# Longformer attention into a softplus layer: weights loaded in smaller pieces, the first batch's loads and the engines' sequence rearranged

## The chip, the core and the metric

The kernel runs on one core of one Trainium2 chip. The metric is the device time of the kernel in microseconds (us), median of three runs. Lower is better.

## What is computed

The reference is attention with a window and eight global positions, followed by two dense layers with a softplus between them. Cut to what matters:

```python
# q, k, v: [8 batches, 8 heads, 576 positions, 64], fp32
mask = np.abs(pos[:, None] - pos[None, :]) <= 32
mask = mask | is_global[:, None] | is_global[None, :]
scores = np.where(mask, q @ k.T / 8, -1e9)
attn = softmax(scores)
x = (attn @ v).transpose(0, 2, 1, 3).reshape(4608, 512)
g = softplus(x @ w_in)        # w_in  [512, 2048]
out = g @ w_out               # w_out [2048, 512], fp32 out
```

## The kernel before

**Tiles.** The 576 positions of a batch are 18 blocks of 32. Four blocks make a pair `n` (36 in all), four pairs make a tile `m` of 512 tokens (nine in all). For each pair TensorE computes the scores `s` (32 small matmuls on a divided array, L1085), the softmax runs on VectorE, ScalarE and GpSimd and ends in `pt`, the transposed probabilities (L1149). For each tile TensorE then computes `xo` (L1259: probabilities by values, and by `vg`, the global rows' part), which is copied to `xT` in bf16, and the dense layers `h` (L1294: 64 matmuls of 512 columns a tile) and `o` (L1305). The first tile is cut into three pieces of one, two and one pair, so that `h` starts on 128 tokens as soon as pair 0 is through. Work that is done once per batch: turning q and k (`tr`), choosing the global positions (`pick`), their scores `sg`, and `ov`, which gives `vg`.

**The start.** For the first batch, q and k come in parts (L522 full parts of 256 tokens, L526 the tail of 64 tokens in two transfers) on SyncE's queue. The values `vb` (L477, eight transfers) and the weights `w_in` (`weights_in`, L1356, eight transfers into four tiles `win0` to `win3`) and `w_out` (`weights_out`, L1360, four) go through GpSimd's queue, because they are cast to bf16 on the way. A transfer that is issued by an engine is an instruction in that engine's queue. Three gates order these transfers: `T["held"]` (L1373) is a one-element copy on GpSimd that waits for a part of q, so that `w_in` comes behind it; `follow` (L765) is a tiny transfer `trail` on SyncE that reads the last element of a weight tile and so waits for it, ahead of the second batch's parts (`win2`) and values (`wout0`); `T["landed"]` (L1437) is a copy that waits for a part of the second batch's k, ahead of `w_out`.

**The sequence.** A class `_Order` plans all work. The table `ORDER` fixes which job comes next and on which engine; the planner's constants (`SWITCH`, `SLOW`, `FETCH`, the `moves` of a transfer) give each job a planned time, by which the jobs of all engines are sorted when they are written out. Where TensorE has a planned gap in the first 34 us, `keep` fills it with matmuls on zeros (`warm`, L737). The planner also knows that TensorE's instructions are fetched in blocks:

```python
    BLOCK = 256
    ASK = 130
    NEED = 448
```

It takes it that a block of 256 instructions is asked for when instruction 130 (386, 642, ...) is reached and is needed at instruction 448 (704, 960, ...).

**The table of picks** (`make_pick`, L595 to L603) is used from the third batch on: VectorE clears it, makes three small tables and compares four times (L601).

## Time and profile before

| | |
|---|---|
| median of 3 runs | 331.63 us (331.45 to 332.01) |
| the profiled execution | 331.16 us, of which its span (first to last instruction) is 329.1 us |
| TensorE busy | 319.9 us (97%) |
| ScalarE, VectorE, GpSimd busy | 233.8, 219.9, 196.0 us |
| TensorE's granted clock, mean over the span | 0.995 |
| `warm` matmuls | 46 |

All times in the rows count from the first instruction of the span. PE is TensorE's matmuls, PEld its weight loads, DVE VectorE, ACT ScalarE, POOL GpSimd, SP SyncE; a small q behind a name is the engine's sequencer. In the chain of waits, "issue" is time in which the engine waited for nothing that the profile shows. Matmuls overlap, so a busy TensorE isn't one at its peak: start times show its pace.

### The profile page before, as it was taken

The numbers are of one execution on the slowest core, as the hardware profiler recorded it, in microseconds if no ns is written. First come the engines' busy times: TensorE is split into PE (matmuls) and PEld (weight loads), VectorE is DVE, ScalarE is ACT, GpSimd is POOL, SyncE is SP. The second block draws the span as 40 slices with busy tenths as digits, with TensorE's granted clock in tenths as the row PEclk, the third lists the DMA queues.
The fourth block names the chain that finished last, engine by engine and source line by source line (L and its number), as shares of the span: only waits on it lengthen the run. The fifth ranks groups of instructions, "written<-read, shape, count | busy, mean of one in ns | idle before, by whom it ended". The sixth has DMA issues, their size and how long they took to land.

```text
span 329.1 us, 12101 instructions
## 1 busy us (share of the span) xinstructions
PE 319.9 (97%) x5290; PEld 171.3 (52%) x5290; DVE 219.9 (67%) x386; ACT 233.8 (71%) x459; POOL 196.0 (60%) x175
## 2 busy tenths in 40 slices
PE   8878999999999999999999999999999999999996
PEld 3536876565555444544555445445544454454444
DVE  7796689847997799884995975378776970431000
ACT  5698879676798896488558857995749647914622
POOL 7827828996678567969587496738282927230000
PEclk9997999999999999999999999999999999999999
DMA  7998999999889899999999960370010012001002
GB/s 193 187 205 195 198 189 155 157 166 244 136 152 146 152 226 173 180 228 189 178 179 167 155 162 4 127 145 3 4 66 0 36 66 85 13 32 66 34 32 97
DMA packets 168796, 42.14 MB, mean 128 GB/s; under 512 B 153256, under 2 KB 165800, under 8 KB 168744
## 3 DMA queue, kind: packets, MB, share of 16 engines
q1 hardware_dynamic: 155928, 27.15, 46.8%
q0 software_dynamic: 10944, 11.08, 16.9%
q10 hardware_dynamic: 1872, 3.15, 2.5%
q8 instruction: 41, 0.67, 0.9%
q14 instruction: 11, 0.09, 0.1%
HBM read 36.71 MB, written 9.44 MB: 140 GB/s over the span
## 4 chain that ended last, share of the span: by engine, by line
PE 90%; DVE 2%; SPq 2%; DMA 2%; issue 1%; ACT 1%
PE o L1305 39%; PE h L1294 37%; PE xo L1259 4%; PE s L1085 4%; DMA stage<-in_q_dram 2%; PE ov L1005 2%; SPq L522 1%; PE pick L894 1%; SPq L526 1%; PE sg L976 1%; PE warm L737 1%; DVE qx L728 1%; PE tr L865 1%; DVE m L1100 1%; PE pick L907 1%
## 5 line engine op out<-in xcount | busy, mean ns | idle before, releaser
L1305 PE MATMUL o<-wout,g 128*128 128x512 bf16 (+1 forms) x592 | 138.3, 374 | 0.0
L1294 PE MATMUL h<-xT,win 128*128 128x512 bf16 (+3 forms) x768 | 137.8, 328 | 0.1
L1300 ACT ACTIVATE g<-h 128x512 bf16<-128x512 f32 (+3 forms) x192 | 84.5, 503 | 30.0 <-PE h L1294 27.0
L1140 POOL TENSOR_TENSOR pn<-st,rs 128x1024 bf16<-128x1024 f32 (+1 forms) x38 | 66.7, 1766 | 55.7 <-DVE rs L1134 49.9
L1294 PEld LDWEIGHTS <-win 128*128 128x128 bf16 x768 | 67.5, 99 | 59.6 <-issue 0.8
L1305 PEld LDWEIGHTS <-g 128*128 128x128 bf16 x592 | 55.9, 98 | 60.7 <-ACT g L1300 1.0
L1108 POOL TENSOR_TENSOR st<-st,m 128x1024 f32<-128x1024 f32 x32 | 60.2, 1894 | 27.1 <-DVE m L1102 27.0
L1089 DVE TENSOR_TENSOR st<-s,mask 128x512 f32<-128x512 f32 x64 | 41.1, 677 | 18.6 <-PE s L1085 18.4
L1132 DVE TENSOR_REDUCE sm<-st 128x8 f32<-128x1024 f32 x32 | 38.5, 1203 | 14.8 <-ACT st L1125 14.6
L1102 DVE TENSOR_REDUCE m<-st 128x8 f32<-128x1024 f32 x32 | 37.9, 1209 | 0.3
L728 ACT COPY osb<-o 128x512 f32<-128x512 f32 (+1 forms) x30 | 17.2, 577 | 22.6 <-PE o L1305 20.2
L1125 ACT ACTIVATE st<-st 128x1024 f32<-128x1024 f32 x32 | 32.7, 1052 | 0.3
L1149 DVE STREAM_TRANSPOSE pt<-pn 128x512 int32<-128x512 int32 x36 | 24.5, 690 | 5.2 <-POOL pn L1140 5.1
L728 ACT CAST xT<-xo 128x512 bf16<-128x512 f32 (+3 forms) x28 | 11.7, 467 | 18.8 <-PE xo L1259 18.8
L728 DVE CAST xT<-xo 128x512 bf16<-128x512 f32 (+3 forms) x20 | 11.3, 601 | 17.5 <-PE xo L1259 17.4
L1300 ACT ACT_TABLE_LOAD x15 | 19.2, 1283 | 1.7 <-PE h L1294 1.5
L1125 ACT ACT_TABLE_LOAD x14 | 18.0, 1283 | 0.7 <-ACT osb L728 0.4
L725 POOL TENSOR_SCALAR qb<-stage 128x1152 bf16<-128x1152 f32 (+2 forms) x15 | 16.8, 1126 | 2.2 <-issue 1.1
L1085 PE MATMUL s<-kx,qx 64*32 64x128 bf16 x1152 | 14.5, 220 | 3.6 <-issue 2.8
L1085 PEld LDWEIGHTS <-qx 64*32 64x32 bf16 x1152 | 10.4, 90 | 12.2 <-issue 8.9
L728 POOL CAST vb<-stage 128x1152 bf16<-128x1152 f32 x12 | 13.7, 1146 | 3.3 <-DMA stage<-in_v_dram 3.3
L737 PE MATMUL warm<-vb 128*128 128x512 bf16 x46 | 13.9, 451 | 1.3 <-DVE vb L559 1.3
(127 smaller groups left out, 287.2 us busy)
## 6 DMA issues: line engine op xcount, KB each, us to landing
stage<-in_v_dram SPq DMA_DIRECT2D x56, 144.0 KB, 4.2
stage<-in_q_dram SPq DMA_DIRECT2D x48, 144.0 KB, 3.7
stage<-in_k_dram SPq DMA_DIRECT2D x48, 144.0 KB, 4.0
out_dram<-osb POOLq DMA_DIRECT2D x24, 256.0 KB, 3.2
out_dram<-osb ACTq DMA_DIRECT2D x11, 256.0 KB, 2.0
stage<-in_q_dram SPq DMA_DIRECT2D x4, 512.0 KB, 6.2
stage<-in_k_dram SPq DMA_DIRECT2D x4, 512.0 KB, 6.9
win<-in_moe_w_in_dram POOLq DMA_DIRECT2D x8, 256.0 KB, 7.7
```

Of the source, the lines that this page charges most:

```text
L728: {"ACT": nc.scalar.copy, "DVE": V.tensor_copy, "POOL": nc.gpsimd.tensor_copy}[e](out, in_)
L1085: nc.tensor.matmul(out=PS["s", n, g][quad(a), x, :], lhsT=qx[b % 2][rows(g), a, j * BL:(j + 1) * BL], rhs=kx[b % 2][rows(g), a, e0 * BL:(e ...
L1089: V.tensor_tensor(out=PS["st", n][:, h, :, :], in0=PS["s", n, h][:, :, :], in1=mask[:, h, j0:j0 + PB, :, :].rearrange("p j s i -> p j (s i ...
L1102: V.reduce_max(out=m[:], in_=flat(PS["st", n], h0, h1), axis=AX)
L1108: on(e).tensor_tensor(out=t, in0=t, in1=over(PS["m", n, y][:], SL * BL), op=OP.subtract)
L1125: nc.scalar.activation(out=t, in_=t, func=AF.Exp)
L1132: V.reduce_sum(out=sm[:], in_=flat(PS["st", n], h0, h1), axis=AX)
L1140: on(e).tensor_tensor(out=PS["pn", n][:, :, :, h0:h1].rearrange("p x s h -> p h x s"), in0=PS["st", n][:, h0:h1], in1=PS["rs", n, y][:].re ...
L1149: V.transpose(out=bass.AP(base.tensor, base.offset, ap=[list(base.ap[0]), [2 * STEP, PB // 2], [STEP + BL // 2, 2], [1, SL * BL]]), in_=PS ...
L1294: nc.tensor.matmul(out=h[:, :], lhsT=w_in_t[c // 4][:, kd, c % 4 * P:(c % 4 + 1) * P], rhs=PS["xT", m][:, kd, lo:hi], start=(kd == 0), sto ...
L1300: nc.scalar.activation(out=PS["g", m, c][:, lo:hi], in_=PS[key][:, lo_of(c, hi - lo)], func=AF.Softplus)
L1305: nc.tensor.matmul(out=PS["o", m, ns, a][:, :], lhsT=PS["g", m, kf][:, ns * P:(ns + 1) * P], rhs=w_out_t[kf // 4][:, kf % 4, a:z], start=( ...
```

## The change

1. `w_in` comes in sixteen transfers of half the rows, `w_out` in eight.
2. The table of picks is made in five pieces, four of which (`make_picks`) can stand apart.
3. The gate ahead of the second batch's parts waits for the second of `win2`'s four transfers (before: for the second of its two); the gate ahead of `w_out` waits for the first full part of the second batch's k and no longer for the second.
4. The planner's constants differ, and with them the planned times and the places of the `warm` matmuls. `ORDER` is a new table.

The diff, cut to its core:

```diff
-    SWITCH = 107
+    SWITCH = 96
...
-    FETCH = 4000
-    SLOW = ((27000, 8000), (34500, 6200), (55000, 8200), (230000, 6000), (1e9, 4500))
+    FETCH = 5500
+    SLOW = ((27000, 6000), (36500, 5800), (60000, 6500), (118000, 5500), (152000, 6500), (230000, 5500), (1e9, 5000))
+    CAP = 6500
...
-    ORDER = (52, 57, 62, 162, 167, 122, 137, 146, 156, 4, 117, 113, 151, 141, 132, 127, 182, 172, 177, 187, 370, 9, 14, 213,
...
+    def make_picks(r):
+        V.tensor_tensor(out=pick[quad(r)].rearrange("p c e g -> p (c e) g")[:, :, r * NG:(r + 1) * NG],
...
-        nc.sync.dma_start(out=trail[x:x + 1, :], in_=t[D:D + 1, t.shape[1] - 1, t.shape[2] - 2:])
+        nc.sync.dma_start(out=trail[x:x + 1, :], in_=t[row:row + 1, t.shape[1] - 1, t.shape[2] - 2:])
...
-                    follow(0, w_in_t[2])
+                    follow(0, w_in_t[2], 0)
...
-    def weights_in(x, y):
-        nc.gpsimd.dma_start(out=w_in_t[x][rows(y), :, :],
-                            in_=moe_w_in[y * HG * D:(y + 1) * HG * D, x * WC:(x + 1) * WC].rearrange("(c d) f -> d c f", d=D))
+    def weights_in(x, y, z):
+        at = (y * HG + z * HG // 2) * D
+        nc.gpsimd.dma_start(out=w_in_t[x][rows(y), z * HG // 2:(z + 1) * HG // 2, :],
+                            in_=moe_w_in[at:at + HG // 2 * D, x * WC:(x + 1) * WC].rearrange("(c d) f -> d c f", d=D))
...
+    def weights_out(a, z):
+        at = (a * 4 + z * 2) * P
+        nc.gpsimd.dma_start(out=w_out_t[a][:, z * 2:z * 2 + 2, :],
+                            in_=moe_w_out[at:at + 2 * P, :].rearrange("(a p) m -> p a m", p=P))
...
-            T["landed"] = o.add(pool(100), lambda e: nc.gpsimd.tensor_copy(seen[:, 0, :], natural(1, 1)[:, 0, 0, 0, 0:1]), [T["part", 1, 1, 1]], rank=0)
+            T["landed"] = o.add(pool(100), lambda e: nc.gpsimd.tensor_copy(seen[:, 0, :], natural(1, 0)[:, 0, 0, 0, 0:1]), [T["part", 1, 1, 0]], rank=0)
```

**SyncE's queue at the start.** `stage_60` is where q lands, `stage_61` k; 64x4x64 is a tail, 128x8x128 a full part. Before:

```order
L531 DMA gi<-in_global_idx_dram 128x16
L522 DMA stage_60<-in_q_dram 128x8x128
L522 DMA stage_61<-in_k_dram 128x8x128 x2
L522 DMA stage_60<-in_q_dram 128x8x128
L526 DMA stage_61<-in_k_dram 64x4x64 x2
L526 DMA stage_60<-in_q_dram 64x4x64 x2
L765 DMA trail<-win_126 1x2x1
L522 DMA stage_61<-in_k_dram 128x8x128 x2
```

Now:

```order
L534 DMA gi<-in_global_idx_dram 128x16
L525 DMA stage_60<-in_q_dram 128x8x128
L529 DMA stage_61<-in_k_dram 64x4x64 x2
L525 DMA stage_61<-in_k_dram 128x8x128 x2
L525 DMA stage_60<-in_q_dram 128x8x128
L529 DMA stage_60<-in_q_dram 64x4x64 x2
L769 DMA trail<-win_126 1x2x1
L525 DMA stage_60<-in_q_dram 128x8x128 x2
L525 DMA stage_61<-in_k_dram 128x8x128 x2
```

The tail of k has moved ahead of k's full parts, and the second batch starts with q.

**GpSimd's queue from its casts of q to the first softmax products.** `pn` is a pair's normalised probabilities. Before:

```order
L665 MEMSET mask 128x9x32 x4
L725 TENSOR_SCALAR qb<-stage_60 128x2x4x64
L477 DMA vb_66<-in_v_dram 32x18x64 x8
L1373 COPY seen<-stage_60 128x1
L1356 DMA win_124<-in_moe_w_in_dram 64x4x512 x2
L671 COPY mask<-mask 128x2x256
L1356 DMA win_125<-in_moe_w_in_dram 64x4x512 x2
L1356 DMA win_126<-in_moe_w_in_dram 64x4x512 x2
L1356 DMA win_127<-in_moe_w_in_dram 64x4x512 x2
L1140 TENSOR_TENSOR pn<-st,rs 128x512 x6
```

Now:

```order
L729 TENSOR_SCALAR qb<-stage_60 128x2x4x64
L669 MEMSET mask 128x9x32 x4
L729 TENSOR_SCALAR qb<-stage_60 128x2x4x64
L480 DMA vb_66<-in_v_dram 32x18x64 x6
L1379 COPY seen<-stage_60 128x1
L1361 DMA win_124<-in_moe_w_in_dram 64x2x512 x2
L480 DMA vb_66<-in_v_dram 32x18x64 x2
L1361 DMA win_124<-in_moe_w_in_dram 64x2x512 x2
L1361 DMA win_125<-in_moe_w_in_dram 64x2x512 x4
L1361 DMA win_126<-in_moe_w_in_dram 64x2x512 x4
L1361 DMA win_127<-in_moe_w_in_dram 64x2x512 x4
L1144 TENSOR_TENSOR pn<-st,rs 128x512 x3
```

Two of the values' transfers now stand behind the first two of `w_in`, a second cast of q has come ahead of all transfers, and three of the six `pn` are gone from here (VectorE has them).

**TensorE where its instruction 704 stands.** Before, the first row here is instruction 702, inside the scores of pair 3:

```order
L1085 MATMUL s<-kx_70,qx_68 32x128
L1085 LDWEIGHTS qx_68
L1085 MATMUL s<-kx_70,qx_68 32x128
L1085 LDWEIGHTS qx_68
L1085 MATMUL s<-kx_70,qx_68 32x128
L1245 LDWEIGHTS vb_67
```

Now, the first row is instruction 700:

```order
L741 MATMUL warm<-vb_67 128x512
L741 LDWEIGHTS vb_67
L741 MATMUL warm<-vb_67 128x512
L1249 LDWEIGHTS vb_67
L1249 MATMUL xo<-vb_67 128x128
L1249 LDWEIGHTS vb_67
```

Instruction 704 is now the first matmul of `xo`, behind all scores of pair 3 and three `warm` matmuls. Instruction 386 was a score matmul of pair 1 and is now the first of `sg`. Over the whole program TensorE has 10,580 instructions where it had 10,582, with 45 `warm` matmuls for 46; from the first `h` on both have 9,767, three `warm` matmuls among them. In that stretch TensorE goes from whole-array matmuls to a divided array 39 times before and 43 times now.

## Rows read from the trace of the kernel before

**Rows 1.** The page: busy time of the engines (share of the span), shares of the chain.

```profile
PE 319.9 (97%) x5290; PEld 171.3 (52%) x5290; DVE 219.9 (67%) x386; ACT 233.8 (71%) x459; POOL 196.0 (60%) x175
...
PE 90%; DVE 2%; SPq 2%; DMA 2%; issue 1%; ACT 1%
```

**Rows 2.** Busy time by stretch: stretch and its length; each engine's busy us; granted clock, DMA.

```profile
23.30:26.14 2.84, 0.00 (x2) 0.00 (x1) 2.13 (x8) 2.84 (x17) 0.62 (x1) 1.00 1.16 194
...
26.48:29.89 3.41, 3.41 (x70) 2.51 (x68) 1.91 (x6) 2.38 (x14) 3.08 (x4) 0.50 0.72 195
28.20:326.00 297.80, 297.40 (x4884) 159.64 (x4882) 197.45 (x317) 213.57 (x387) 177.94 (x134) 1.00 0.63 123
```

**Rows 3.** The chain that ended last: start, length, what.

```profile
22.96 0.34 PE s L1085 x30
23.30 2.84 issue
26.14 0.23 PE s L1085 x2
```

**Rows 4.** DMA queues: all of the run, then 17.8 to 23.8 us, then 23.8 to 24.8 us.

```profile
q8 instruction: 41, 0.67, 0.9%
...
q0 software_dynamic: 1255, 1.20, 122.7%
...
q8 instruction: 1, 0.02, 5.6%
```

**Rows 5.** Timeline, VectorE and ScalarE up to the first `xo`: start, length, engine, what, idle before.

```profile
15.07 0.39 DVE L723 TENSOR_SCALAR qb<-stage 128x256 bf16<-128x256 f32 x1 [0.22 <-DMA stage<-in_q_dram]
...
17.12 0.73 DVE L728 COPY qx<-tr 128x512 bf16<-128x512 bf16 x1
...
24.60 0.71 DVE L1149 STREAM_TRANSPOSE pt<-pn 128x512 int32<-128x512 int32 x1
...
16.14 0.37 ACT L1121 ACTIVATE st<-s,m 128x128 f32<-128x128 f32 x1
...
24.64 0.40 ACT L1016 ACTIVATE vg<-ov,grs 128x128 bf16<-128x128 f32 x1
```

**Rows 6.** Timeline, from pair 0's scores to the end of the first `h`.

```profile
14.85 0.46 PE L1085 MATMUL s<-kx,qx 64*32 64x128 bf16 x32
...
17.04 0.42 PE L1085 MATMUL s<-kx,qx 64*32 64x128 bf16 x32
...
26.30 0.48 PE L1245 MATMUL xo<-vb 128*128 128x128 bf16 x4
...
27.50 0.60 ACT L728 CAST xT<-xo 128x128 bf16<-128x128 f32 x3 [1.07 <-PE xo L1259]
...
28.20 4.33 PE L1294 MATMUL h<-xT,win 128*128 128x128 bf16 x60
...
32.36 0.81 PE L737 MATMUL warm<-vb 128*128 128x512 bf16 x3
```

**Rows 7.** One line's instructions: `w_in` (ns min/median/max, first and last start), its time to landing.

```profile
L1356 POOL DMA_DIRECT2D win<-in_moe_w_in_dram x8: 611/636/668, 12.3 to 17.7; - x8
...
DMA to landing us min/median/max: 6.0/7.7/10.1
```

**Rows 8.** Timeline and waits of GpSimd around `w_in`.

```profile
12.31 0.64 POOL L1356 DMA_DIRECT2D win<-in_moe_w_in_dram  x1 [0.35 <-DMA vb<-in_v_dram]
...
25.52 4.04 POOL L1140 TENSOR_TENSOR pn<-st,rs 128x512 bf16<-128x512 f32 x4 [7.11 <-DVE rs L1134]
```

**Rows 9.** Timeline and chain: pace of whole-array matmuls, and going into a divided array.

```profile
126.54 2.98 PE L1305 MATMUL o<-wout,g 128*128 128x512 bf16 x13
129.45 0.80 PE L1005 MATMUL ov<-vb,pgt 32*32 32x129 bf16 x72
...
271.71 7.77 PE h L1294 x36
```

**Rows 10.** Timeline: the first `o`.

```profile
45.65 0.38 PE L1305 MATMUL o<-wout,g 128*128 128x512 bf16 x1
```

More of the change, by code (lines that the diff above doesn't have):

```diff
@@ L58, in stall @@
                 ask = due.pop(0)
-                took_ = max(next(x for until, x in self.SLOW if ask < until), self.backlog(ask + 1200) - ask + 2400)
+                took_ = max(next(x for until, x in self.SLOW if ask < until), min(self.backlog(ask + 2800) - ask, self.CAP) + 2400)
                 last = max(ask + took_, last + self.FETCH)
@@ L142, in settle @@
                 sent.append(self.PACKETS[job["units"]])
-            self.backs.append((t, now))
+            if q:
+                self.backs.append((t, now))
             done[q] += 1
@@ L172, in keep @@
         if t0 < self.COLD:
-            span = (t1 - t0) * self.LONG
+            span = (t1 - t0) * 0.93
             cold = min(span, self.COLD - t0)
@@ L287, in run @@
                 mine = "POOL" if "POOL" in j["cost"] else "SP"
-                dma.append((mine, t + 1500 if j["cost"][e][0] else t, j["moves"], j))
+                dma.append((mine, t + (1900 if mine == "POOL" else 1500) if j["cost"][e][0] else t, j["moves"], j))
                 j["at"] = t
@@ L759, with follow @@
     followed = set()
-    def follow(x, t):
+    def follow(x, t, row):
         if x in followed:
@@ L795, in emit @@
                 if b:
-                    follow(0, w_in_t[2])
+                    follow(0, w_in_t[2], 0)
                 load_part(b, w, t)
-            T["part", b, w, t] = o.add({"DMA": (700 if b else 0, 0)}, emit, had(("w_in", 2)) + T["cast", 0, w] if b else [], rank=0,
-                                       moves=(1800 if b else 1900) if t < FULL else 900 if b else 650, units=1 if t < FULL else 2)
+            T["part", b, w, t] = o.add({"DMA": (700 if b else 0, 0)}, emit, had(("w_in", 2, 0)) + T["cast", 0, w] if b else [], rank=0,
+                                       moves=1800 if t < FULL else 900 if b else 650, units=1 if t < FULL else 2, late=0 if t < FULL or b else 700)
     def add_cast(b, w):
@@ L1042, in add_global @@
             ovs.append(o.add({"PE": (72 * n, 72 * n + 170) if b else (110 * n + 100, 110 * n + 240)}, lambda e, m0=m0, m1=m1: ov(e, m0, m1), [tps[-1], *ovs, *T["cast", b, 2]],
-                             rank=3, array=32, ins=16 * n, opens=[] if ovs else [("ov", ("ov", b, y)) for y in range(two)], uses=[("ov", b, y) for y in range(two)] if ovs else []))
+                             rank=3, array=34, ins=16 * n, opens=[] if ovs else [("ov", ("ov", b, y)) for y in range(two)], uses=[("ov", b, y) for y in range(two)] if ovs else []))
         T["gexp", b], T["tpg", b], T["ov", b] = exps[-1], tps[-1], ovs[-1]
@@ L1275, in add_values @@
             last = o.add({"PE": (t, t + 170)}, lambda e, s0=s0, s1=s1: val(e, s0, s1), ready if last is None else [last] + (had(("gv", 0)) if ahead else []),
-                         rank=1, array=64, urgent=last is None, ins=16 * (s1 - s0) + (8 if ahead and s0 == 0 else 0), opens=opened if last is None else [],
+                         rank=1, array=65, urgent=last is None, ins=16 * (s1 - s0) + (8 if ahead and s0 == 0 else 0), opens=opened if last is None else [],
                          uses=[("pt", m)] + ([("xo", v_, r) for r in range(KD)] if last is not None else []))
@@ L1375 @@
         for y in range(2):
-            last = T["w_in", x] = o.add({"POOL": (650, 0)}, lambda e, x=x, y=y: weights_in(x, y), [last or T["held"]],
-                                        rank=-1 if x else 0, hold=2000 if x else 0, moves=1340)
+            for z in range(2):
+                last = T["w_in", x] = T["w_in", x, y] = o.add({"POOL": (650, 0)}, lambda e, x=x, y=y, z=z: weights_in(x, y, z), [last or T["held"]],
+                                                              rank=-1 if x else 0, moves=680)
     setup("make_neg", lambda e: make_neg(), pool(1250), [], rank=0)
@@ L1436 @@
             make_batch(1)
-            T["landed"] = o.add(pool(100), lambda e: nc.gpsimd.tensor_copy(seen[:, 0, :], natural(1, 1)[:, 0, 0, 0, 0:1]), [T["part", 1, 1, 1]], rank=0)
+            T["landed"] = o.add(pool(100), lambda e: nc.gpsimd.tensor_copy(seen[:, 0, :], natural(1, 0)[:, 0, 0, 0, 0:1]), [T["part", 1, 1, 0]], rank=0)
             for a in range(KF // 4):
-                T["w_out", a] = o.add({"POOL": (800, 0)}, lambda e, a=a: weights_out(a),
-                                      [T["landed"], T.get(("w_out", a - 1))], rank=-1, hold=800 if a else 0, moves=2700)
+                for z in range(2):
+                    T["w_out", a] = o.add({"POOL": (760, 0)}, lambda e, a=a, z=z: weights_out(a, z),
+                                          [T["landed"], T.get(("w_out", a), T.get(("w_out", a - 1)))], rank=-1, moves=1350)
         for x in range(len(VALS)):
```

25 lines of the change are left out of this document (11 added, 14 removed), and 143 rows, old and new, of the table ORDER.

## The prediction

> **What bounds the kernel now.** Read the page first: TensorE is busy 97% of the span and makes up 90% of the chain of waits [rows 1]. A busy share of an engine whose matmuls overlap doesn't say that nothing is to be gained, so I cut the span at the first `h`, which starts at 28.20 [rows 6]. From there to 326.00 TensorE is busy 297.40 of 297.80 us [rows 2]: it hardly waits, and both programs have the same 9,767 instructions in that stretch. So the change can act in two ways: on **when the first `h` starts**, and on **what TensorE loses after it**.
>
> Ahead of the first `h` the chain shows one piece that is no work at all: 30 of the 32 score matmuls of pair 3, then 2.84 us of "issue", then the last two [rows 3]. TensorE does nothing in 23.30 to 26.14, while VectorE and ScalarE go on [rows 2]. This is the fetch of instructions. The page's instruction queue carried 41 packets in 0.67 MB [rows 4], so some 16 KB for every 258 of the 10,582 instructions; TensorE stops behind instruction 704, where the planner's constants say that a block is needed; and one packet of that queue moves in 23.8 to 24.8, none of it in the 6 us before, in which GpSimd's queue moved 1.20 MB [rows 4]. That block is asked for at instruction 386, in the scores of pair 1, at about 17.2 [rows 6], and serves 8.9 us later. What lay in front of it is `w_in`: eight transfers issued from 12.31 to 17.7, which land 6.0 to 10.1 us after their issue [rows 7, 8].
>
> The stall has a second price. The granted clock is 0.50, the lower of the two levels, 1.2 GHz, from 26.48 to 29.89 [rows 2], after the idle stretch. The first 16 matmuls of `h` take (29.90 - 28.20) / 16 = 106 ns each, the other 44 up to 32.36 take 56 ns [rows 6]: 16 x 50 ns = 0.8 us lost.
>
> **The change, part by part.**
>
> *The stall.* Instruction 704 is now the first matmul of `xo`. TensorE has to wait there anyway, for `pt` of pair 0 and then for `vg`. Before, these two were there at 25.31 and 25.04 [rows 5], 1.0 us ahead of the `xo` that came at 26.30 [rows 6]. So of the 2.84 us only about 1 us was the stall's own. Instruction 386 is now the first of `sg`, at about 16.4 to 17.4. By then GpSimd, which issues halves and has two of the values' transfers between them, has fewer bytes of `w_in` in the queues. I take the block as there in time: even with the 8.9 us of before it would serve at 25.3 to 26.3.
>
> *The chain to `vg`.* ScalarE now has 24 exponential steps ahead of `vg` where it had 20. Between its first (16.14) and `vg` (24.64) [rows 5] stand 20 of them and about 1 us for the global rows: (8.50 - 1.0) / 20 = 0.37 us each, so 4 more cost 1.4 us. Against that, pair 0's scores start earlier than 14.85 [rows 6]. They need all of k, whose tail has moved to the front of SyncE's queue; and the exponentials came behind the tail of q, which VectorE waited for until 15.07 [rows 5] and which now meets two transfers fewer of the values. I can't read how much earlier: 0 at the least; at the most 1.7 us, by adding the casts and copies in their new order. I take 1.2 us, nearer to the upper end, because VectorE's cast of k's tail and one of its copies no longer stand ahead of the scores. VectorE alone gives no less: it gains the same start, and gets a `qx` tail (about half of 0.73 us [rows 5]) and a `kx` copy (0.7 us) between scores and `pt`. So `vg` ends at 25.04 + 1.4 - 1.2 = 25.2; bounds 24.7 and 26.4.
>
> *From `vg` to the first `h`.* The last matmuls of `xo` and the cast of `xT` (27.50 to 28.10 [rows 6]) make some 1.2 us. The first `h` is then at 26.5 (bounds 25.9 to 27.6): **-1.7 us**, and between -2.3 and -0.6.
>
> *The clock.* TensorE now waits between the three `warm` matmuls and `xo`, some 1.5 to 2 us instead of 2.84. No row shows whether the clock falls after a wait of that length; I take it that it stays: **-0.8 us**, with 0 at the other end.
>
> *Divided arrays.* TensorE goes into a divided array 43 times after the first `h`, before 39 times. 13 matmuls of 512 columns and the step into `ov` take 129.45 - 126.54 = 2.91 us; 36 such matmuls in a row take 7.77, 0.216 each [rows 9]. So a step costs 2.91 - 13 x 0.216 = 0.10 us, and four more **+0.4 us**.
>
> *The transfers.* Eight more of `w_in` and four more of `w_out` cost GpSimd at most 0.64 us each for `w_in` [rows 7], 5 us; it has 7.11 us of idle time between the last `w_in` and `pn` [rows 8]. That cover goes nearly whole: with the two transfers of values behind the first of `w_in`, GpSimd should be through at 22 to 23.7, `pn` of pair 1 can start at about 24. The last columns of `w_in` land where they did (17.7 + 10.1 = 27.8 [rows 7]) or 0.6 us later, as the bytes are the same and the queues were full; the 49th `h`, which needs them, comes at 26.5 + 2.7 = 29.2. `w_out`'s gate opens one part of k earlier, well ahead of the first `o` (45.65 [rows 10]).
>
> The Trainium skill (DMA: Bandwidth & Descriptors, "Rules for kernel authors") tells to join small transfers to large ones, at best 1 MiB and more, which speaks against halving them; by its fit of 2.0 us and the bytes, sixteen of them end to end would be an estimated 16 us longer in fixed costs. The trace doesn't agree that they stand end to end: 1.20 MB in 6 us is a steady stream [rows 4].
>
> *The table of picks* is four instructions of VectorE that may stand apart, used from the third batch on; VectorE is busy for 67% [rows 1]: nothing.
>
> *New waits after the first `h`.* Before, 0.4 us [rows 2]. In the new order the exponentials of pair 3, a table load and seven softplus steps stand ahead of ScalarE's cast for the second piece, which I make some 0.5 us late. I take **+0.6 us**, between 0 and 3.
>
> Sum: -1.7 - 0.8 + 0.4 + 0.6 = **-1.5 us**. The profiled execution took 331.16 us, so 329.7; the median of the runs lies 0.47 us above it, so I say **330.1 us**.
>
> **The rivals.**
>
> *The clock falls all the same, or the stall comes back in front of `xo`.* For it: the wait stays at 1.5 us and more, and all was bound to the same transfers. Against: the wait is half as long. The 0.8 us aren't won, and `xo` runs at half pace, 0.4 us: -1.5 + 1.2 = -0.3, 331.3 us. The Trainium skill (Runtime: NRT & Kernel Launch, "Instruction fetch mechanics") says that crossing a block costs one bump of the queue's tail and is mostly hidden; by that the 2.84 us would be something else that a change of transfers needn't remove. The trace speaks against it with its packet at 23.8 to 24.8.
>
> *The whole chain moves.* If scores start 1.7 us earlier and ScalarE catches up, the first `h` is at 25.9 and no new wait comes: -2.3 - 0.8 + 0.4 = -2.7, with some luck 328.7 us.
>
> *GpSimd is held by `w_in`.* Its first transfer waited for a landing of the values [rows 8]: an issue waits until an earlier transfer is done. Sixteen of them wait more often, and all `pn` of pairs 1 and 2 stand behind the last, in order. Three `pn` of 1.0 us [rows 8] must be done when `h` of the first piece ends, at about 29.5, less two transposes of 0.7 us: they must start by 25. From 27.1 on the change loses; at 28 the clock falls too: -1.5 + 3.0 + 0.8 = +2.3, 333.9 us.
>
> *Halves cost as much as wholes.* Landings lie (27.8 - 18.3) / 7 = 1.36 us apart [rows 7]. If each half took that, the sixteenth would land at 18.3 + 15 x 1.36 = 38.7 and the 49th `h` wait some 8 us behind `xo`: 337.6 us. The steady stream of bytes speaks against it.
>
> **How the numbers follow.** Forecast 0.45; clock or stall 0.25; whole chain 0.12; GpSimd held 0.14; halves 0.04. A measurement of this kernel can tell 0.2%, 0.66 us, from no change. Forecast and whole chain are faster: 0.57; clock or stall is the same: 0.25; the last two are slower: 0.18. The forecast's own range is 329.3 to 331.0. For 8 in 10 I go down to 328.5, which takes in most of the whole chain, and up to 332.6, which takes in the second case and the mild half of GpSimd's.
>
> **What would show it.** Right: no "issue" piece near 23 us; a packet of the instruction queue well before 24; granted clock 1.00 throughout; the first `h` near 26.5 and its matmuls at 56 ns from the start; idle time after it about 1 us. Wrong: a first `h` later than 27.6; the clock at 0.50 around it; `pn` on GpSimd starting after 25; TensorE waiting for `pt`, `xT` or `win` between 29 and 50.

## The result, and the profile after

The changed kernel takes **335.62 us** (median of 4 runs, 334.45 to 337.25), the kernel before 331.65 on the same chip: a ratio of 1.0122 with a 95% interval of 1.0078 to 1.0166. It is 4.0 us **slower**; the forecast was 330.1 us, its range ended at 332.6. The profiled execution took 335.38 us, with a span of 333.7.

The page of the changed kernel, busy time by engine and the chain that ended last, to be set beside [rows 1]:

```profile
PE 318.4 (95%) x5289; PEld 169.4 (51%) x5289; DVE 227.8 (68%) x401; ACT 229.8 (69%) x448; POOL 202.8 (61%) x185
...
PE 81%; DMA 8%; DVE 4%; POOL 2%; ACT 2%; SPq 1%; issue 1%; ACTq 0%
```

TensorE's busy time fell by 1.5 us and its share of the chain from 90% to 81%: what came in are transfers, 8% for 2%. Where they stand in the run the stretches tell, as in [rows 2] (stretch and length; busy us of PE, PEld, DVE, ACT, POOL; granted clock, DMA share, GB/s):

```profile
23.96:26.39 2.43, 0.38 (x2) 0.00 (x0) 1.72 (x8) 2.06 (x12) 0.73 (x3) 1.00 1.15 176
26.48:29.89 3.41, 3.09 (x82) 2.42 (x83) 2.62 (x5) 2.48 (x15) 3.39 (x4) 1.00 1.08 183
27.91:330.19 302.28, 297.58 (x4884) 158.49 (x4882) 206.29 (x331) 210.77 (x378) 182.09 (x138) 1.00 0.61 122
```

Three readings. The idle piece ahead of `xo` is still there: 2.06 us for 2.84 by the profile's idle time, or 2.43 for 3.05 from the start of one matmul to the start of the next (this second measure is used below for the waits ahead of `xo`). The clock stayed at 1.00, 2.4 GHz, through the stretch that ran at 0.50 before. And from the first `h` to the last matmul it now takes 302.28 us for 297.80, with the same 4,884 matmuls and nearly the same busy time, although the slow clock of before is gone: **4.7 us of TensorE waiting in the one part of the program that had 0.4**. The first `h` itself starts at 27.91 where it was 28.20 [rows 6].

The timeline of TensorE has the larger waits (start, length, what; in brackets the idle time ahead and what the profile takes to have ended it). From `xo` to the scores of the second batch, as in [rows 6]:

```profile
26.39 0.40 PE L1249 MATMUL xo<-vb 128*128 128x128 bf16 x4 [2.06 <-ACT vg L1020]
...
27.91 0.50 PE L1298 MATMUL h<-xT,win 128*128 128x128 bf16 x6
28.74 2.50 PE L1298 MATMUL h<-xT,win 128*128 128x128 bf16 x42 [0.32 <-DMA win<-in_moe_w_in_dram]
31.74 0.32 PE L1263 MATMUL xo<-pt,vg 32*64 32x256 bf16 x8 [0.50 <-DVE rs L1138]
...
44.41 0.54 PE L1089 MATMUL s<-kx,qx 64*32 64x128 bf16 x32 [0.86 <-DVE kx L732]
```

and from the first `o`, which started at 45.65 before [rows 10], to 61 us:

```profile
47.78 0.38 PE L1309 MATMUL o<-wout,g 128*128 128x512 bf16 x1
...
50.95 1.90 PE L1309 MATMUL o<-wout,g 128*128 128x512 bf16 x8 [1.92 <-ACT g L1304]
...
55.78 0.81 PE L1309 MATMUL o<-wout,g 128*128 128x512 bf16 x3 [0.21 <-DVE st L1093]
...
60.92 1.04 PE L1309 MATMUL o<-wout,g 128*128 128x512 bf16 x4 [0.59 <-ACT g L1304]
```

With a wait of 0.29 us at 37.51, the idle times from 28 to 61 us add up to the 4.7; behind 61 us no single wait of TensorE is above 0.2 us. So the loss lies between 28 and 61 us. Two of these labels deceive: the waits that end at 26.39 (`<-ACT vg`) and at 50.95 (`<-ACT g`) end with fetches of instructions. The packet of TensorE's instruction queue, q8, shows it. It is there in the first and the last of three windows, and in the 6.8 us ahead of the last there is only another instruction queue's (queue: packets, MB, share):

```profile
q8 instruction: 1, 0.02, 5.8%
...
q14 instruction: 1, 0.01, 0.3%
...
q8 instruction: 1, 0.02, 5.6%
```

The windows are 23.85 to 24.95, 41.65 to 48.45 and 48.45 to 49.50. Before, TensorE went on at 26.14 [rows 3], 1.42 us after its packet had ended at 24.72. Now it goes on at 26.39 and 50.95, 1.48 and 1.51 us after packets that ended at 24.91 and 49.44 (the ends are those of the packets' records in the trace). The waits stand at instructions 704 and 1728, whole blocks apart (4 x 256). The small wait at 37.51 is a third of the kind, at instruction 1216 and 1.42 us after its packet.

GpSimd and `w_in`, as in [rows 7, 8] (one line's instructions, the time to landing, then the timeline):

```profile
L1361 POOL DMA_DIRECT2D win<-in_moe_w_in_dram x16: 578/615/756, 13.3 to 26.3; - x16
...
DMA to landing us min/median/max: 4.3/5.9/7.2
...
26.27 0.58 POOL L1361 DMA_DIRECT2D win<-in_moe_w_in_dram  x1 [1.59 <-DMA win<-in_moe_w_in_dram]
26.86 3.04 POOL L1144 TENSOR_TENSOR pn<-st,rs 128x512 bf16<-128x512 f32 x3
```

A half costs GpSimd as much as a whole did (615 ns for 636). The last is issued at 26.3 for 17.7 and lands at 26.27 + 4.94 = 31.2 for 27.8; `pn` starts at 26.86 for 25.52.

Last, VectorE in the stretch in question, a row that the forecast had no counterpart for:

```profile
43.44 0.30 DVE L598 TENSOR_TENSOR pick<-posK,gf 32x144 bf16<-32x144 f32 x1
...
47.59 1.22 DVE L1106 TENSOR_REDUCE m<-st 128x8 f32<-128x1024 f32 x1
48.84 0.30 DVE L598 TENSOR_TENSOR pick<-posK,gf 32x144 bf16<-32x144 f32 x1
49.15 1.22 DVE L1106 TENSOR_REDUCE m<-st 128x8 f32<-128x1024 f32 x1
50.29 4.12 DVE L598 TENSOR_TENSOR pick<-posK,gf 32x144 bf16<-32x144 f32 x2
54.44 1.89 DVE L1093 TENSOR_TENSOR st<-s,mask 128x512 f32<-128x512 f32 x3
```

Four equal pieces of the table of picks: 0.30, 0.30, 0.77 and **3.34 us** (the last from 51.07 to 54.41). GpSimd, meanwhile:

```profile
48.90 2.00 POOL L1112 TENSOR_TENSOR st<-st,m 128x1024 f32<-128x1024 f32 x1 [4.21 <-DVE m L1106]
50.85 1.45 POOL L1366 DMA_DIRECT2D wout<-in_moe_w_out_dram  x2
52.33 1.91 POOL L1112 TENSOR_TENSOR st<-st,m 128x1024 f32<-128x1024 f32 x1
```

Its two subtractions end at 50.90 and 54.24; the two slow pieces end 0.16 and 0.17 us later. Before, the four stood in one go at 40.06 and took 1.56 us, and one of them was held even there: 0.62 us, to 40.99, behind this cast of GpSimd's, which ended at 40.83:

```profile
40.16 0.67 POOL L725 TENSOR_SCALAR qb<-stage 128x512 bf16<-128x512 f32 x1
```

### The profile page after: what moved, and what is told of

The parts are those of the page before. It is cut to its first block, busy times and chain, and to the rows that moved or that the text cites. A ratio compares the mean times of both kernels' runs of the same rounds, so it can differ in the third digit from the quotient of the medians.

```text
span 333.7 us, 12095 instructions
## 1 busy us (share of the span) xinstructions
PE 318.4 (95%) x5289; PEld 169.4 (51%) x5289; DVE 227.8 (68%) x401; ACT 229.8 (69%) x448; POOL 202.8 (61%) x185
## 4 chain that ended last, share of the span: by engine, by line
PE 81%; DMA 8%; DVE 4%; POOL 2%; ACT 2%; SPq 1%; issue 1%; ACTq 0%
PE o L1309 37%; PE h L1298 34%; PE xo L1263 4%; PE s L1089 3%; DMA stage<-in_k_dram 2%; DMA win<-in_moe_w_in_dram 2%; DMA vb<-in_v_dram 2%; PE ov L1009 2%; DVE pick L598 1%; DMA stage<-in_q_dram 1%; DVE st L1093 1%; POOL win L1361 1%; PE pick L898 1%; SPq L525 1%; DVE m L1106 1%; PE sg L980 1%
## 5 line engine op out<-in xcount | busy, mean ns | idle before, releaser
L1304 ACT ACTIVATE g<-h 128x512 bf16<-128x512 f32 (+3 forms) x192 | 83.0, 509 | 33.0 <-PE h L1298 31.2
L1298 PEld LDWEIGHTS <-win 128*128 128x128 bf16 x768 | 66.8, 98 | 60.1 <-issue 0.7
L1144 POOL TENSOR_TENSOR pn<-st,rs 128x1024 bf16<-128x1024 f32 (+1 forms) x35 | 63.7, 1826 | 44.6 <-DVE rs L1138 38.2
L732 ACT COPY osb<-o 128x512 f32<-128x512 f32 (+1 forms) x24 | 13.6, 567 | 25.0 <-PE o L1309 18.6
L732 POOL CAST vb<-stage 128x1152 bf16<-128x1152 f32 x13 | 14.8, 1145 | 8.7 <-DMA stage<-in_v_dram 4.7
L732 DVE CAST xT<-xo 128x512 bf16<-128x512 f32 (+3 forms) x22 | 10.6, 507 | 10.4 <-PE xo L1263 10.3
L729 POOL TENSOR_SCALAR qb<-stage 128x1152 bf16<-128x1152 f32 (+2 forms) x13 | 15.6, 1205 | 2.5 <-DMA stage<-in_q_dram 2.4
L732 ACT CAST kb<-stage 128x512 bf16<-128x512 f32 (+2 forms) x11 | 10.8, 1006 | 5.8 <-DMA stage<-in_k_dram 5.8
```

Source lines behind the costliest of these rows:

```text
L732: {"ACT": nc.scalar.copy, "DVE": V.tensor_copy, "POOL": nc.gpsimd.tensor_copy}[e](out, in_)
L1144: on(e).tensor_tensor(out=PS["pn", n][:, :, :, h0:h1].rearrange("p x s h -> p h x s"), in0=PS["st", n][:, h0:h1], in1=PS["rs", n, y][:].re ...
L1298: nc.tensor.matmul(out=h[:, :], lhsT=w_in_t[c // 4][:, kd, c % 4 * P:(c % 4 + 1) * P], rhs=PS["xT", m][:, kd, lo:hi], start=(kd == 0), sto ...
L1304: nc.scalar.activation(out=PS["g", m, c][:, lo:hi], in_=PS[key][:, lo_of(c, hi - lo)], func=AF.Softplus)
```

## The experiments

Three theories went through them. **F**: the fetch of instruction blocks, late behind the new mix of transfers. **P**: the pieces of the table of picks beside GpSimd. **Q**: the new sequence itself. (Other letters are explained where the expectations use them.) Each ratio is to runs of the kernel before on the same chip; there that kernel had medians of 332.2 to 332.9 and a spread of 330.0 to 337.5, so ratios are read, not differences to 331.65. The rows of a run come from one execution of it, and its other executions can differ (the changed kernel's mean granted clocks do, 0.995 to 1.000); only the ratios stand on several.

**1. The halves.** `w_in` whole in the changed kernel (and in the same way `w_out`, and both), and `w_in` in halves in the kernel before:

```
 def weights_in(x, y, z):
-    at = (y * HG + z * HG // 2) * D
-    nc.gpsimd.dma_start(out=w_in_t[x][rows(y), z * HG // 2:(z + 1) * HG // 2, :], ...
+    if z == 0:
+        nc.gpsimd.dma_start(out=w_in_t[x][rows(y), :, :], ...
```

> The changed kernel with w_in in eight whole transfers again, each issued where the first of its two halves stood; all else as changed. Theory A (starved queue: one issue of GpSimd costs some 0.6 us whatever its size, so halves of 128 KB can feed at most some 210 GB/s, which is what the queues move, and any other transfer between them leaves the queues empty): the last w_in lands by 28.5 instead of 31.2, the gate of the second batch opens near 25.5, most of the 4.0 us come back: 331.5 to 333. Theory B (the new sequence itself: values begun 2 us later, 24 exponentials ahead of vg, the gate): landing moves little and the time stays at 334.5 to 336.5. Theory C (w_out in halves holds up the block of instructions at 48.8): 335 to 336, with the wait of 2.1 us at 48.8 still there.

> The changed kernel with w_out in four whole transfers, each issued where its first half stood; w_in stays in halves. Theory A: within 1 us of the changed kernel's 335.6. Theory C: the wait at 48.8 goes, 333 to 334. Theory B: 335 to 336.

> The changed kernel with w_in and w_out both whole: the new sequence without any of the halves. Theory A: as with w_in whole alone, 331 to 333. Theory C: 333 to 334 or less. Theory B: 334.5 or more, with the first h near 28 and new waits at 43 and 48 still there.

> The kernel before with w_in in sixteen halves, nothing else changed: each issue becomes two, one right behind the other. Theory A: GpSimd issues until 24 or later instead of 18.4, pn starts no earlier, the last w_in lands 1 us or more later than 27.8, and the time rises by 1 to 3 us, to 332.6 to 334.6. Theory B: its values are all issued before w_in, so the same bytes land as before and the time stays within 0.7 us of 331.65.

Ratios 1.0117 (1.0057 to 1.0177), 1.0100 (1.0037 to 1.0163), 1.0135 (1.0080 to 1.0191) and 1.0018 (0.9985 to 1.0051). **The halves cost nothing that can be told**: whole again, the changed kernel stays 1.0 to 1.4% slower, and halves in the kernel before leave it where it was. Theory A of these expectations, the starved queue, is right about the queue and wrong about the time. With `w_in` whole, the last issue began at 18.8 and the last landing came at 28.2, 3 us earlier than with halves; the time did not follow. The idle piece ahead of `xo` was there in all four, 1.8 to 3.0 us long, so a late landing could hide behind it; no run has `w_in` whole and this block in time.

**2. Blocks of instructions.** 50 more matmuls (100 instructions) in the first `warm` group, in both kernels; 12 of 512 columns stay, and small ones of 8 columns, which take 1.8 us, make up the rest:

```
+        wide = n if filled else 12
+        filled.append(key)
-        for x in range(n):
+        for x in range(wide):
             nc.tensor.matmul(out=ps[:, 0:w], ...
+        for x in range(50 + n - wide if wide < n else 0):
+            nc.tensor.matmul(out=ps[:, 0:8], lhsT=idle[:, 0, :], rhs=idle[:, 0, 0:8], ...
```

> The changed kernel with 50 more matmuls (100 instructions) ahead of the first real work, in the time in which TensorE waits for q and k: the first group of warm matmuls has 12 of 512 columns and 64 of 8 columns in place of 26 of 512. Theory F (the waits of 2.4 us ahead of xo and of 2.1 us at 48.8 are the fetch of a block of instructions that stands behind other transfers): blocks end at fixed counts of instructions, so both waits leave their places by 100 instructions: the second block is asked for near 15 instead of 17.2, comes before 24, and xo then waits for vg alone: first h at 27.0 to 27.6; no wait of 2 us in front of the o at 48.8, though one may stand 100 instructions ahead of it; time 333 to 335. Theory S (the new sequence: xo waits for pt and vg, o for g): both waits stay at the same instructions with their lengths, time 335.6 within 0.7.

> The kernel before with the same 50 more matmuls in its first group (12 of 512 columns and 67 of 8 in place of 29). Theory F: the idle stretch of 2.84 us between the scores of pair 3 goes or shortens to 1 us, xo starts when pt is there (25.4), the granted clock stays at 1.00 and the first h comes at 26.5 to 27.5 instead of 28.2: time 329.5 to 331 by its own profile, unless another block's wait appears in 40 to 60. Theory S: the wait stays in 23.3 to 26.1, the time within 0.5 us of the kernel before.

Both waits left their places, as F said. In the changed kernel with the pad, `xo` and the first `h`:

```profile
25.80 0.49 PE L1269 MATMUL xo<-pt,vb 32*64 32x64 bf16 x40 [0.35 <-DVE pt L1159]
...
27.30 0.45 PE L1304 MATMUL h<-xT,win 128*128 128x128 bf16 x4
...
35.40 0.40 PE L1304 MATMUL h<-xT,win 128*128 128x128 bf16 x4 [2.15 <-issue]
...
50.54 1.89 PE L1315 MATMUL o<-wout,g 128*128 128x512 bf16 x8
```

The block that held up `xo` had come at 19.06; the `o` that waited 2.1 us doesn't wait. But new waits stand at other blocks, and the time is far off what I expected: 1.0466 (1.0422 to 1.0510) for the changed kernel and 1.0352 (1.0302 to 1.0402) for the one before, **11 to 12 us each from 100 more instructions** in time in which TensorE had no other work. The stretches of the changed kernel with the pad show why (same columns as above; the last row is the stretch at the end of the second wait):

```profile
33.10:35.30 2.20, 0.15 (x3) 0.00 (x0) 2.17 (x6) 0.69 (x5) 0.00 (x0) 1.00 1.16 294
144.00:146.70 2.70, 0.14 (x16) 0.00 (x0) 1.29 (x2) 2.68 (x4) 1.73 (x2) 0.98 0.87 156
179.90:182.50 2.60, 0.29 (x2) 0.01 (x1) 0.00 (x0) 2.60 (x5) 2.60 (x4) 1.00 0.03 6
213.00:215.20 2.20, 0.16 (x21) 0.06 (x7) 0.00 (x0) 0.00 (x0) 0.52 (x1) 0.93 0.00 0
...
146.62:150.03 3.41, 3.20 (x23) 1.19 (x23) 2.71 (x3) 0.67 (x1) 0.82 (x1) 0.50 1.12 219
```

The waits are not all of it. From the first `h` on TensorE's idle times add up to 12.7 us for 4.7, and the granted clock was 0.50 in three stretches of 3.4 us: the one in the last row and those from 57.87 and 214.88, each at or behind a wait (of 2.7, 1.6 and 2.2 us of idle time). Two of the four waits come with hardly any transfers under way (6 and 0 GB/s): there the block is late because it is asked for late. Between asking (130 + 256 n instructions, by the planner's constants) and needing (448 + 256 n, where the waits stand) lie 318 instructions. In whole-array matmuls of 512 columns that is 159 x 0.216 [rows 9] = 34 us; in a run of small divided ones it was 1.5 us (142.4 to 143.9), less than any fetch of the changed kernel took (2.1 us and more). In both kernels as they are no such wait shows there, and shifting every block's end by 100 brings them. I had not thought of that when I wrote the expectation. It can be worked out: asks and needs shifted by 100 along the changed kernel's own trace, with its own fetch times, give waits, behind the first ten blocks, at 21, 25 and 29, and these three appeared.

Then fewer instructions instead of more:

```
-        for x in range(n):
+        for x in range(18 if n == 26 else n):
```

> The changed kernel with 18 instead of 26 matmuls in its first warm group, so 16 instructions less ahead of every block's end. Theory F, worked out by shifting asks and needs by 16 instructions along the changed kernel's own trace and taking each block's measured time from asking to packet plus 1.45 us: the wait at 48.8 falls from 2.1 to about 0.9 us, the one ahead of xo stays near 2.3, the later blocks stay without a wait; time 1 to 1.5 us less than the changed kernel, 334.0 to 334.8. If the waits come from the engines: no change, 335.6 within 0.7.

1.0158 (1.0099 to 1.0216). The wait at 48.8 went, in front of `xo` too (the block came in 5.4 us), and a new one of 1.6 us came at block 37, again without transfers under way. And still not faster, for where the blocks were in time, this came:

```profile
26.13 0.44 PE L1298 MATMUL h<-xT,win 128*128 128x128 bf16 x4
27.41 0.27 PE L1298 MATMUL h<-xT,win 128*128 128x128 bf16 x2 [0.84 <-DMA win<-in_moe_w_in_dram]
28.04 1.16 PE L1298 MATMUL h<-xT,win 128*128 128x128 bf16 x18 [0.35 <-DMA win<-in_moe_w_in_dram]
...
49.64 1.89 PE L1309 MATMUL o<-wout,g 128*128 128x512 bf16 x8
...
55.92 0.38 PE L1298 MATMUL h<-xT,win 128*128 128x128 bf16 x4 [1.93 <-DVE st L1093]
```

**What stood behind the late blocks were `w_in` at the first `h` and, at 50 to 56, VectorE.** Part 4 is about VectorE. First, what makes a block late:

```
 def weights_in(x, y):
+    if (x, y) == (2, 0):
+        nc.gpsimd.tensor_copy(seen[0:D, 1, :], qg[0][0:D, 0, 0:1])
```

> The kernel before with one more gate on GpSimd: the fifth of the eight w_in transfers waits, by a copy of one column of qg to seen, until VectorE has written qg (17.1), so half of w_in is issued after the block for 26.14 was asked for at 17.19. Theory F (the block stands behind the transfers issued before it): its packet comes near 22.7 instead of 23.8, TensorE goes on near 25.0 instead of 26.14, xo follows when pt is there, the clock stays at 1.00; w_in lands as before, since its stream doesn't break; first h at 26.5 to 27.5, time 0.8 to 1.7 us less than before. Rival (the block waits for a share of the engines, not for its turn): packet at 23.5 to 24.5 as before, time the same or up to 1 us longer by the later w_in.

0.9991 (0.9957 to 1.0025): no change. Four of the eight `w_in` transfers instead of six had been issued when the block was asked for at 17.27, and its packet ended at 24.77 for 24.72. So the block does not simply stand behind what was issued before it: that reading of mine falls. What sets its 7.5 us stays open.

**3. Starts and gates.**

```
a_values   casts[0]["on"] = "ACT"; all eight transfers of values ahead of the gate
a_gate     follow(0, w_in_t[2], 0)  ->  follow(0, w_in_t[1], 0)
b_gates    before: trail reads row 0; seen reads natural(1, 0) for natural(1, 1)
```

> The changed kernel with GpSimd's queue begun as before: one of its two casts of q goes to ScalarE, and all eight transfers of values stand ahead of the gate and of w_in. Theory L (late start of the values and of w_in): the values start near 7 instead of 8.1, the last w_in lands 1 to 1.5 us earlier than 31.2, and the time falls by 1 to 2 us. Theory F: w_in's stream is only earlier in front of the same fetch, the block for xo still ends at 23.5 to 25 and the first h stays at 27 to 28.5; time 335 to 336.

> The changed kernel with the gate of the second batch's loads on the second column block of w_in in place of the third. Theory L2 (the second batch is late): the gate opens near 24, its keys have all landed by 37.5 instead of 39.1, the wait of 0.9 us ahead of the scores at 43.3 goes, the time falls by 0.8 to 1.5 us to 334.1 to 334.8. Rival: these loads then run beside the rest of w_in, whose last landing goes from 31.2 to beyond 32.5, and h waits for it near 30: time 335.6 or more.

> The kernel before with the changed kernel's gates alone: the second batch's loads wait for the first half of w_in's third column block (row 0 instead of row 64), and w_out's gate reads the first part of k instead of the second. Theory F and the late second batch: loads start about 1.2 us earlier, w_out 0.5 to 2 us earlier, no wait comes or goes but for the block needed near 47.7, which has 0.2 us to spare: 0 to +2 us, most likely the same within 0.7 us. Rival (the gates are what costs the 4 us): 1.5 us or more slower.

1.0128 (1.0052 to 1.0203) and 1.0111 (1.0058 to 1.0165), two runs each: neither gives anything back. With the earlier gate the first `h` came at 25.91 and stood still for `w_in` soon after (1.21 and 0.36 us), as the rival of that expectation had it. The change's gates alone in the kernel before: 1.0036 (1.0004 to 1.0068), with two blocks late in its profile (1.3 us each, at 36.6 and 48.7).

**4. The table of picks.** The first piece moved behind the copy that fills `kx`; then, from the changed kernel, the last three pieces moved to 44.2, where GpSimd issues a transfer and computes nothing; then two pieces of the kernel before moved to where the changed kernel has them:

```
a_picks         jobs: ("make_picks", 3) behind ("fill", 1)
a_picks_early   jobs: ("make_picks", 0..2) behind ("xev", 2, 1), ahead of the masks
b_picks_late    before: pieces 0 and 2 behind ("mx", 5, 0)
```

> The changed kernel with the first of the four pieces of the table of picks (0.30 us on VectorE at 43.44) behind the copy that fills kx of the second batch instead of ahead of it. Theory (this piece stands in the chain that the scores at 44.4 wait for): that wait falls from 0.93 to about 0.65 us, time 0.2 to 0.4 us less. Rival (the wait is set by the late keys alone): no change.

> The changed kernel with the last three of the four pieces of the table of picks moved ahead of VectorE's four masks of the second batch (to 44.4, where GpSimd is idle until 48.9), from 48.8, 50.3 and 51.1. Theory P (the piece at 51.07 takes 3.34 us instead of 0.30 because it reads two tiles beside GpSimd's subtraction and is let go only when that ends, and the masks behind it hold PSUM that the matmuls of 52 to 60 wait for): all pieces take some 0.3 us, the masks start near 52 instead of 54.4, the waits at 55 and 60 (1.1 us in the changed kernel's profile, 3 to 4 us where the block of 48.8 came in time) go: 1 to 3 us less than 335.6. Theory F alone (the block needed at 48.8 is the cost): no change in the median, within 0.7 us.

> The kernel before with two of the four pieces of the table of picks taken out of their place (40.1) and put where the changed kernel has them, behind the row maxima of pairs 4 and 5 (48.7), beside GpSimd's two subtractions (47.6 to 51.35). Theory P: each piece ends only when a subtraction ends, near 49.6 and 51.5, so VectorE's masks come 1.5 to 2.5 us late and TensorE waits for PSUM: time 1 to 2.5 us more. Rival: the pieces take 0.3 us each, VectorE has 0.9 us of idle time there: no change.

The first alone: 1.0088 (1.0055 to 1.0121). The wait for `kx` fell to 0.1 us, but its last piece took 4.42 us (two pieces in 5.20), and TensorE paid for it, since the sixth block (needed at instruction 1728) was in time here:

```profile
50.01 5.20 DVE L598 TENSOR_TENSOR pick<-posK,gf 32x144 bf16<-32x144 f32 x2
...
55.99 0.38 PE L1298 MATMUL h<-xT,win 128*128 128x128 bf16 x4 [3.02 <-DVE st L1093]
```

The kernel before with two pieces late, VectorE, GpSimd and TensorE:

```profile
48.41 3.02 DVE L605 TENSOR_TENSOR pick<-posK,gf 32x144 bf16<-32x144 f32 x2
51.46 1.29 DVE L1093 TENSOR_TENSOR st<-s,mask 128x512 f32<-128x512 f32 x2
...
47.45 3.81 POOL L1112 TENSOR_TENSOR st<-st,m 128x1024 f32<-128x1024 f32 x2 [6.68 <-DVE m L1106]
...
52.20 1.43 PE L1298 MATMUL h<-xT,win 128*128 128x128 bf16 x20 [1.49 <-DVE st L1093]
```

1.10 and 1.91 us for pieces of 0.30, each let go 0.16 us after one of GpSimd's subtractions; the masks start at 51.46 for 49.53, and 1.0032 (1.0005 to 1.0059) is the price. In the changed kernel with the pieces early each of the three takes 0.30, the masks are back at 51.35, and nothing between 49 and 58 waits:

```profile
44.19 0.92 DVE L598 TENSOR_TENSOR pick<-posK,gf 32x144 bf16<-32x144 f32 x3
45.14 2.48 DVE L1093 TENSOR_TENSOR st<-s,mask 128x512 f32<-128x512 f32 x4
...
51.35 1.89 DVE L1093 TENSOR_TENSOR st<-s,mask 128x512 f32<-128x512 f32 x3 [1.34 <-PE s L1089]
...
60.14 0.79 PE L1009 MATMUL ov<-vb,pgt 32*32 32x129 bf16 x72 [1.05 <-POOL vb L732]
```

1.0075 (1.0046 to 1.0104) for 1.0122: some 1.5 us of the 4.0, though the two intervals overlap, and in this profile the sixth block was in time as well. **That the pieces are held beside GpSimd is shown in both directions, by the rows; what it costs the changed kernel is known only roughly, and it is not all.** In this profile the first `h` is at 28.36, and 300.54 us follow, 2.7 more than before: 0.8 ahead of the second batch's scores, 1.1 at `ov` (the row above), 0.6 at 68 for `xT`. (Its clock was at 0.50 from 25.64 to 29.05, as before.)

**5. Parts or sequence.** All parts in the kernel before with its own sequence (halves, gates, late pieces), and the changed kernel's sequence without them, with either set of gates:

```
b_parts         before + w_in, w_out in halves + gates + pieces 0 and 2 late
a_order         after + w_in, w_out whole + pieces early + gates as before
a_order_gates   after + w_in, w_out whole + pieces early
```

> The kernel before with the changed kernel's parts but not its new sequence: w_in and w_out in halves, its gates, and two pieces of the table of picks beside GpSimd's subtractions. Theory A (the parts cost it, each on its own): the gates alone gave a ratio of 1.0036, the pieces 1.0032, the halves of w_in 1.0018; their sum makes 1.007 to 1.010, 2.3 to 3.3 us. Theory Q (the new sequence of the engines costs most of it): 1.004 or less, since these waits cover each other.

> The changed kernel's sequence alone: w_in and w_out whole, the gates as before (row 64 of w_in's third column block, second part of k), three pieces of the table of picks moved to 44.4. Theory A: near the kernel before plus four steps into a divided array, ratio 1.000 to 1.004. Theory Q: the sequence has q ahead of k in the second batch's loads, so its keys come last (39.1 for 36.7), and 24 exponentials ahead of vg; 1.006 or more.

> As the run with the sequence alone, but with the changed kernel's gates. Theory A: the gates cost 0.3 percent here too, ratio 1.003 to 1.007. Theory Q: the earlier gates help a sequence whose keys are late, so this is 0.2 percent or more faster than the one with the gates as before, 1.005 to 1.008.

1.0029 (1.0006 to 1.0051), 1.0123 (1.0093 to 1.0154) and 1.0076 (1.0036 to 1.0115). That speaks against Theory A: **the parts cost the kernel before 0.3%, which is what its two late pieces cost alone; the new sequence costs 0.8% with its own gates and 1.2% with the old ones.** The earlier gates, 0.4% dear when put alone into the kernel before, look worth 0.5% to the new sequence, whose second batch is late (these two intervals overlap as well). The last of the three and the run with the pieces early differ by the halves alone: 1.0076 and 1.0075. In the profile of the sequence alone the scores of the second batch still wait for `kx`, and the sixth block is late again:

```profile
44.46 0.54 PE L1089 MATMUL s<-kx,qx 64*32 64x128 bf16 x32 [0.67 <-DVE kx L732]
...
50.76 0.60 PE L1309 MATMUL o<-wout,g 128*128 128x512 bf16 x2 [1.13 <-issue]
```

No version beat the kernel before; the best of the changed ones are the two with the pieces early and the new gates.

## Why the prediction was wrong, point by point

**The stall (-1.7, measured -0.3).** The step that failed first is "I take the block as there in time". Asked for at 17.19, it served at 26.39, 9.2 us later. The prediction's own figure spoke against it: by the 8.9 us of before the block would serve at 25.3 to 26.3, up to 1.1 us behind the 25.2 it gave `vg`. What was to close that gap was GpSimd's smaller backlog, and no row said that a smaller backlog brings the packet sooner; in the kernel before it does not (b_hold). The price can be read: where the block is there before `vg` the first `h` comes 0.91 us after `vg` (a_pad, a_less, a_gate), here 1.89 us after it, so the block cost 1.0 us. `vg` itself ended at 26.02 for 25.2, within the bounds: ScalarE's exponentials began 0.77 us earlier than before, not 1.2, and took 1.75 us longer, not 1.4. (In eight of the other eleven profiles of the changed sequence `vg` ended at 24.9 to 25.4.) The last 0.4 us went the other way, as 0.91 us is less than the 1.3 between the forecast's `vg` and `h`.

**The clock (-0.8).** Right in the profiled execution, and by luck: 1.00 from 4.6 us to the last matmul, after a wait of 2.4 us (from start to start) where 3.05 had been followed by 0.50. In the seven other profiles of the changed sequence with a wait of 2.4 us and more ahead of `xo` the clock fell each time, in a_both_whole after 2.5 us; in b_hold, after 2.95, it did not. Of the changed kernel's other three runs two have a mean granted clock of 0.995, that of the kernel before.

**Divided arrays (+0.4).** 43 steps as counted; the pace of `h` and `o` is as before, nothing speaks against the 0.10 us each.

**The transfers (nothing).** "GpSimd should be through at 22 to 23.7", with `pn` at about 24, failed: 26.84 and 26.86, since an issue also waited for an earlier landing (2.2 us in three waits). The last landing came at 31.2 for a forecast of 27.8 to 28.4. This is the first half of the rival that GpSimd is held, which had 0.14, and its mark, `pn` after 25, came. Its second half did not: the wait in front of the second piece's `xo` was 0.5 us and the one for `w_in` 0.3, not 3.0. `w_in` whole again, which took that away, did not make the kernel faster. But where the block came sooner, the late weights showed: `h` stood still for `w_in` for 0.8 us in a_pad, 1.2 in a_less and 1.6 in a_gate. So with the block in time much of the 1.7 us could have gone to this wait. (Not always: in a_out_whole, whose `h` came at 26.6, the last landing was at 29.5 and `h` did not wait.)

**The table of picks (nothing).** Failed. Cover was named by VectorE's 67% busy, an average, and not by what runs beside the pieces. Each reads two tiles in SBUF, and GpSimd's subtraction beside it reads two. The Trainium skill (SBUF — State Buffer, "Who interferes with whom") says that a VectorE instruction with two SBUF inputs and a GpSimd instruction that reads SBUF exclude each other, the later one waiting in full. The traces agree: four held pieces were let go 0.16 to 0.17 us after a subtraction's end, while a piece that started ahead of one (48.84 in the changed kernel) ran at 0.30; by that rule each of the two pieces could be held for up to one subtraction of 1.9 us, an estimate that the rows exceed (3.34 and 4.42). What it costs is about 1.5 us here, roughly, and 1.1 in the kernel before.

**New waits after the first `h` (+0.6, between 0 and 3; measured +5.3 with the 0.4 of the steps in it).** This is the term that turned the sign: the stretch from the first `h` on grew by 4.5 us although the clock gave back its 0.8. By the profile 4.3 us of it is idle time (4.7 for 0.4). It was mis-sized, and looked for in one place. The 0.5 us late cast that the term was made of is not among the waits that came. They are the keys of the second batch, asked for behind q, their full parts landing by 39.1 for 33.6 (0.9 us at 43.3; that the late keys make this wait is my reading, no run moved them alone); the block needed at 48.8 (2.1 us), and where that block is in time, VectorE's masks behind the picks (2 to 3 us): one covers the other, which would explain why removing either alone moved the median little or not at all; small waits at 28 to 38 for `w_in`, for the softmax and for a third block (0.3, 0.5 and 0.3 us); and what stands behind these (0.2 and 0.6 us at 55 and 60). I had compared the order of the engines up to the first `h` and trusted the 0.4 us of idle time of before for the rest. A new sequence does not inherit it.

**The rivals.** The stall in front of `xo` did come back, as in the rival that ended at 331.3. Its price of 1.2 us was made of the slow clock and of `xo` at half pace, and neither came in the profiled execution; that it is near the 1.0 us which the block cost is luck. (The halves' 337.6 leaves out the 0.47 us between profile and median: 330.1 and 8 make 338.1.) Of the two rules of the Trainium skill that were weighed, the one for large transfers (DMA: Bandwidth & Descriptors, "Rules for kernel authors") changed no time here, though each half costs GpSimd as much as a whole one; and what the other says (Runtime: NRT & Kernel Launch, "Instruction fetch mechanics"), that crossing a block is mostly hidden, holds for the count and not for the price: of 41 blocks three were not hidden in the changed kernel's trace, and two of these cost 2.4 and 2.1 us from start to start; where the blocks' ends were moved it was four waits of 2.2 to 2.7 us of idle time.

What stays open: what sets the 5 to 8 us of a fetch beside a steady stream (for the block ahead of `xo` it was 3.5 in a_pad, 5.4 in a_less and 7.1 to 8.5 in fifteen of the nineteen profiles); why the slowest piece was held across an issue of `w_out` as well, when a piece at 43.44 ran at 0.30 beside one; what halves of `w_in` cost once the block is in time; and how the sequence's 0.8% divide, since no run undid the order of q and k in the second batch alone.

## What to carry to other kernels

A small instruction that "may stand anywhere" is priced by what the other engines run beside it at that moment, so list which instructions of VectorE read two tiles in SBUF and see what GpSimd does beside each. Where a program is long enough for blocks of instructions to be fetched, count instructions: a block asked for in a run of short ones is late whatever the transfers do, and 100 instructions more at the start cost 11 us and more, most of it behind 140 us. And when two waits lie on top of each other, removing one may show nothing; put each suspect into the kernel that lacks it as well, as the late pieces in the kernel before did.

## What the runs showed of the hardware that I had not expected

- TensorE stops for a late block of instructions at fixed counts (704, 1216 and 1728 here, 256 apart or a multiple of it), and goes on 1.2 to 1.7 us after the end of its 16 KB packet (1.42, 1.48 and 1.51 in the three waits read first above; the range is that of all such waits in the nineteen profiles). That a block is asked for 318 instructions ahead is the planner's constant; no row shows the asking itself.
- Four of VectorE's 0.30 us instructions were held for 0.77, 1.10, 1.91 and 3.34 us and let go 0.16 to 0.17 us after a subtraction of GpSimd's had ended; one of 0.62 us in the kernel before was let go 0.15 us after a cast of GpSimd's, and the one of 4.42 us in a_picks 0.17 us after a cast that followed the subtraction.
- An issue on GpSimd takes the same time for 128 KB as for 256 KB (615 and 636 ns), which at 128 KB makes 213 GB/s, about what the queues carried before (197 to 210 GB/s from 17 to 23 us); in the changed kernel, with other issues between, they carried 90 GB/s from 19 to 20 us.
- The kernel before had medians of 331.65 to 332.93 in six sets of runs, and single runs of 330.0 to 337.5. What sets that spread is not shown; in its profile the sixth block had some 0.3 us to spare (an estimate: its packet's end at 45.90 and 1.45 us, against 47.62), and with `w_in` in halves it was 2.3 us late.
